# A fused attention and MLP block on one Trainium2 core: another hand-held list for the same program

## The chip, the cores and the metric

The kernel runs on one core of one Trainium2 chip. The metric is the device time of one execution in microseconds (us) on that core; lower is better. Times of several executions are given by their median.

## What is computed

The reference is one pre-norm transformer block on 2048 tokens of width 640, in bfloat16:

```python
x = A_x
h = x + _A_ref(_layernorm(x), A_wq, A_wk, A_wv, A_wo, A_beta)   # attention with a compressive memory
h2 = h + _B_ref(_layernorm(h), B_w1, B_w2)                       # silu MLP, 640 -> 1728 -> 640
```

The attention has 32 heads of 20 elements. The 2048 tokens are cut into 4 segments of 512. Within a segment each head does causal softmax attention; beside it, each query reads a memory matrix M (and its normaliser z) that holds all earlier segments, and the two results are mixed with a gate:

```python
for s in range(4):
    p = softmax(qs @ ks.T * scale + mask);  a_dot = p @ vs
    pq = phi(qs);  a_mem = (pq @ M) / (pq @ z + 1e-06)          # phi(t) = t+1 if t>0 else exp(t)
    outs.append(g * a_mem + (1.0 - g) * a_dot)
    pk = phi(ks);  M = M + pk.T @ vs;  z = z + pk.sum()
```

## The kernel before, in words

The program is a graph of some 1,400 small tasks. Each task is a few instructions of one engine, or one DMA, with the tiles that it reads and writes. `build` declares the tasks segment by segment; `schedule` (line 286) then walks one list, `ORDER` (line 356), and gives each task its place, its engine and its buffer slots. An entry reads `name/engine:slots`: `qe020x/A:0` is task `qe020x` on ScalarE with slot 0 of its pool; without an engine the task's first one is taken. `fill30:7` puts 30 matmuls on zeros into PSUM bank 7 that nothing reads. An entry `e10a+` where another list has `e10a0` and `e10a2` does the exponentials of four heads in one instruction instead of two. Nothing reorders later: each engine executes its instructions in the sequence in which their tasks stand in the list, and `Tracker.add` (line 72) adds the semaphore waits that the data need. The list is therefore the whole schedule. It also sets what is queued behind what on SP, which issues nearly all DMAs one after the other: an entry that waits there holds all that come after it.

The names in the list, with the lines that show in the profile (s is the segment 0 to 3, b the block of 128 tokens 0 to 15):

- `x..` loads tokens (L578), `w_..` loads weights (L581; `w_w1_0` to `w_w1_4` are the five 432 KB rows-blocks of the first MLP weight, `w_w2_0` to `w_w2_5` the second weight).
- `n1_st`, `n1_r`, `n1_ap` are the first layer norm of a block: statistics (L742, L745), reciprocal root (L757 to L763) and apply (L769). `n1_tr` is the DMA that transposes the result into `xT` (L798). `n2_..` is the same for the second norm, into `hT`.
- `pr` projects to q or k (PE, L866), `qe` evicts that from PSUM (L882 on ScalarE, L883 on VectorE), `v`/`ve` are the values (PE L827, eviction L842).
- `ex`, `pha`, `phb` make phi (L889, L896, L902). `vt` and `vp` are DMAs that copy parts of q, k and phi(q) into the layout of three extra head groups (L914, L927). The first segment's q and k, and these copies, lie in the space of the second MLP weight, so the profile calls them `w_sb`.
- `qk` are the scores of four heads (PE, L964), `e` their exponentials (ScalarE, L976), `mk` the causal mask (GpSimd, L987), `av` the product with the values (PE, L1008, in segment 0 L1092), `oe` its eviction, `tn` a turn back to token order plus the read of the memory (PE, L1038, L1042, in segment 0 L1123), `nm` the division (VectorE, L1056 to L1062, in segment 0 L1135 to L1137), `ad` the sum (GpSimd, L1070).
- `kt` transposes phi(k) by DMA (L1207), `kg`/`kh` gather it (L1198), `mz`, `ma`, `mb` update the memory (L1225, L1241, L1249).
- `ot` transposes the attention's output by DMA (L1264), `wo` projects it (PE, L1272), `rs` adds it to the tokens (VectorE, L1280).
- `h1`, `th`, `s` are the MLP's first matmul with silu (PE L1307, in the last partial chunk L1301; ScalarE L1316; VectorE L1322), `h2` the second (PE, L1349), `o` the sum (VectorE, L1362), `out` the store (L1367).

PSUM has 8 banks. A matmul that needs a bank waits until the task that read it last is done, so an eviction that stands late in VectorE's or ScalarE's part of the list can hold TensorE. There are 12 token buffers for 16 blocks: `x12` loads the last four blocks into the buffers of the first four, and so waits for the four stores `out0` to `out3`.

The scores run as four matmuls side by side on 20 rows each (`tile_position=(32 * r, 0)`), the product with the values as four on 32 columns each; everything else uses the whole array. The list interleaves these with projections and MLP matmuls, so TensorE changes between the three forms all through the first 240 us.

The lines that place a task:

```python
for row in ORDER:
    name, _, slots = row.partition(":")
    name, _, eng = name.partition("/")
    ...
    t = todo.pop(name)
    t.eng = {"A": AC, "D": DV, "G": PO, "S": SP}[eng] if eng else list(t.engs)[0]
    ...
        a.slot = slots.pop(0)
    ...
    order.append(t)
```

## Time and profile before

| what | value |
|---|---|
| median of 3 runs | 298.06 us (297.7 to 300.65) |
| the profiled execution | 298.33 us, its span 296.6 us |
| TensorE busy | 285.0 us, 96% of the span, 2991 matmuls |
| VectorE, ScalarE, GpSimd busy | 222.8, 217.5, 139.9 us |
| mean granted TensorE clock | 1.000 |
| moved by DMA | 25.40 MB, mean 86 GB/s |

The span is the time from the first to the last instruction; the 1.7 us between it and the execution's own time lie around the program. In the chain of waits each line is a start, a length and what ran or was waited for. In the list of waits a line reads: engine, line and tile that waited, what released it, then total us, number of times, longest. In the instruction rows, the two numbers ahead are start and length, and what stands in brackets is the engine's idle time just before with its releaser. Two matmuls overlap in the profile, so their pitch is read from one start to the next.

### The profile page before, as it was taken

The numbers are of one execution on the slowest core, as the hardware profiler recorded it, in microseconds if no ns is written. First come the engines' busy times: TensorE is split into PE (matmuls) and PEld (weight loads), VectorE is DVE, ScalarE is ACT, GpSimd is POOL, SyncE is SP. The second block draws the span as 40 slices with busy tenths as digits, with TensorE's granted clock in tenths as the row PEclk, the third lists the DMA queues.
The fourth block names the chain that finished last, engine by engine and source line by source line (L and its number), as shares of the span: only waits on it lengthen the run. The fifth ranks groups of instructions, "written<-read, shape, count | busy, mean of one in ns | idle before, by whom it ended". The sixth has DMA issues, their size and how long they took to land.

```text
span 296.6 us, 7437 instructions
## 1 busy us (share of the span) xinstructions
PE 285.0 (96%) x2991; PEld 167.6 (56%) x2991; DVE 222.8 (75%) x506; ACT 217.5 (73%) x266; POOL 139.9 (47%) x257
## 2 busy tenths in 40 slices
PE   7897879999999999999999999999999999999997
PEld 5775445545665455566643444465665457764575
DVE  3897889768989789899678967759967688626522
ACT  5875979999999899999879999788759751014400
POOL 6246834744656477646525656355576620200000
PEclk9999999999999999999999999999999999999999
DMA  7968772804943321254462400154181023220002
GB/s 208 366 209 114 192 105 68 221 18 98 168 89 75 74 39 26 37 111 66 97 140 51 77 1 2 26 75 88 20 102 32 0 59 76 68 67 25 22 22 91
DMA packets 49906, 25.40 MB, mean 86 GB/s; under 512 B 39488, under 2 KB 48032, under 8 KB 49872
## 3 DMA queue, kind: packets, MB, share of 16 engines
q1 hardware_dynamic: 48204, 23.18, 37.3%
q10 hardware_dynamic: 1668, 1.74, 1.9%
q8 instruction: 24, 0.39, 0.6%
q14 instruction: 10, 0.08, 0.1%
HBM read 10.41 MB, written 2.62 MB: 44 GB/s over the span
## 4 chain that ended last, share of the span: by engine, by line
PE 76%; DVE 8%; DMA 7%; ACT 4%; POOL 2%; issue 2%; SPq 1%; DVEq 0%; ACTq 0%
PE ps_all L1349 19%; PE ps_all L1307 15%; PE ps_all L866 12%; PE ps_all L1272 7%; PE ps_all L964 7%; PE ps_all L827 5%; PE ps_all L1008 5%; ACT PT L976 3%; DMA x_tok<-in_A_x_dram 3%; DMA xT<-xn_rot 2%; PE ps_all L1038 1%; DMA w_sb<-w_sb 1%; PE ps_all L1092 1%; PE ps_all L1225 1%; POOL PT L987 1%
## 5 line engine op out<-in xcount | busy, mean ns | idle before, releaser
L976 ACT ACTIVATE PT<-ps_all 128x1024 bf16<-128x1024 f32 (+1 forms) x120 | 153.1, 1310 | 17.7 <-PE ps_all L964 16.5
L987 POOL TENSOR_SCALAR_AFFINE_SELECT PT<-PT 128x512 bf16<-128x512 bf16 x128 | 81.5, 647 | 59.1 <-ACT PT L976 57.0
L1349 PE MATMUL ps_all<-w_sb,sT 128*128 128x320 bf16 (+2 forms) x462 | 64.9, 295 | 0.0
L1307 PE MATMUL ps_all<-hT,w_sb 128*128 128x512 bf16 (+1 forms) x325 | 63.0, 337 | 0.5 <-DVE sT L1322 0.4
L1316 ACT ACTIVATE th<-ps_all 128x512 f32<-128x512 f32 (+2 forms) x70 | 34.0, 505 | 35.1 <-PE ps_all L1307 31.0
L1349 PEld LDWEIGHTS ps_all<-w_sb,sT 128*128 128x128 bf16 x462 | 43.2, 98 | 18.3 <-issue 1.8
L1322 DVE SCALAR_TENSOR_TENSOR sT<-th,ps_all 128x512 bf16<-128x512 f32 (+2 forms) x70 | 37.8, 561 | 17.1 <-ACT th L1316 16.1
L1307 PEld LDWEIGHTS ps_all<-hT,w_sb 128*128 128x128 bf16 x325 | 29.8, 98 | 25.9 <-issue 3.2
L763 POOL TENSOR_TENSOR rst<-rst,eps_c 128x1 f32<-128x1 f32 x32 | 18.4, 579 | 25.1 <-DVE rst L757 23.5
L742 DVE BATCH_NORM_STATS2 stt<-x_tok 128x6 f32<-128x320 bf16 x62 | 27.2, 481 | 1.8 <-DMA x_tok<-in_A_x_dram 1.4
L1362 DVE SCALAR_TENSOR_TENSOR x_tok<-ps_all,x_tok 128x640 bf16<-128x640 f32 (+3 forms) x18 | 13.3, 745 | 16.7 <-PE ps_all L1349 16.6
L1070 POOL TENSOR_TENSOR otok<-on 128x320 bf16<-128x320 bf16 x24 | 19.0, 796 | 11.5 <-DVE on L1062 11.5
L1272 PE MATMUL ps_all<-wo_sb,oT 128*128 128x320 bf16 x160 | 23.8, 299 | 0.0
L883 DVE CAST QK<-ps_all 128x512 bf16<-128x512 f32 x23 | 15.7, 688 | 8.8 <-PE ps_all L866 8.7
L1062 DVE TENSOR_TENSOR on<-ps_all,rd 128x640 bf16<-128x640 f32 x24 | 19.8, 825 | 0.9
L827 PE MATMUL ps_all<-wv_sb,xT 128*128 128x320 bf16 x120 | 18.3, 299 | 1.6 <-DMA xT<-xn_rot 1.3
L1272 PEld LDWEIGHTS ps_all<-wo_sb,oT 128*128 128x128 bf16 x160 | 15.0, 98 | 7.2 <-issue 1.8
L866 PE MATMUL ps_all<-xT,wkr 128*128 128x512 bf16 x75 | 18.7, 380 | 0.0
L866 PE MATMUL ps_all<-xT,wqr 128*128 128x512 bf16 x75 | 18.2, 380 | 0.0
L842 DVE CAST Vx<-ps_all 128x640 bf16<-128x640 f32 x15 | 12.3, 819 | 5.9 <-PE ps_all L827 5.8
L1008 PE MATMUL ps_all<-PT,Vx 128*32 128x512 bf16 (+3 forms) x384 | 16.4, 301 | 0.1
L769 DVE TENSOR_SCALAR xn_rot<-x_tok,mvt,rst 128x640 bf16<-128x640 bf16 x32 | 14.8, 473 | 1.7 <-POOL rst L763 1.0
(106 smaller groups left out, 338.3 us busy)
## 6 DMA issues: line engine op xcount, KB each, us to landing
w_sb<-in_B_w_dram SPq DMA_DIRECT2D x5, 432.0 KB, 6.1
x_tok<-in_A_x_dram SPq DMA_DIRECT2D x3, 640.0 KB, 8.4
w_sb<-in_B_w_dram SPq DMA_DIRECT2D x3, 480.0 KB, 4.4
out_dram<-x_tok ACTq DMA_DIRECT2D x8, 160.0 KB, 1.8
out_dram<-x_tok SPq DMA_DIRECT2D x7, 160.0 KB, 2.0
QKV<-QK SPq DMA_DIRECT2D x12, 72.0 KB
wo_sb<-in_A_wo_dram SPq DMA_DIRECT2D x1, 800.0 KB, 10.0
sT<-in_A_wq_dram SPq DMA_DIRECT2D x2, 320.0 KB, 4.3
```

The source lines that it names most:

```text
L742: T.add(DV, lambda e, hh=hh: e.bn_stats(out=stt[:, s, 6 * hh:6 * hh + 6], in_=xb[:, 320 * hh:320 * hh + 320]), reads=R((xa, xsub)), writes ...
L827: fns.append(lambda e, c=c, hh=hh: e.matmul(bank(ps, hh)[:, 0:320], lhsT=xT_[:, c, 128 * i:128 * i + 128], rhs=wv_sb[:, c, 320 * hh:320 * ...
L866: fns = [lambda e, kc=kc: e.matmul(bank(ps)[:, lo:hi], lhsT=wt[:, kc, c, :], rhs=xT_[:, kc, lo:hi], start=(kc == 0), stop=(kc == NC - 1)) ...
L964: fns.append(lambda e, j=j, o=o, r=r, q0=q0, q1=q1, qa=qa, ka=ka: e.matmul(ps_all[:, o:o + q1 - q0], lhsT=ka[32 * r:32 * r + DH, 128 * j:1 ...
L976: T.add(AC, lambda e: e.activation(out=pt[:, pta.slot, q0:q0 + nq, 0:width], in_=sc3[:, b0:b0 + nq, 0:width], func=ACT.Exp, scale=SCALE), ...
L987: T.add(PO, lambda e: e.affine_select(out=v, in_=v, pattern=[[0, 4], [1, 128]], compare_op=ALU.is_ge, fill=0.0, base=0, channel_multiplier ...
L1008: fns.append(lambda e, j=j, r=r, h=h, pa=pa, pt=pt, co=co, q0=q0, ji=ji: e.matmul(bank(po)[32 * r:32 * r + 32, q0:hi], lhsT=Vx[:, vx.slot, ...
L1272: fns.append(lambda e, c=c, hh=hh: e.matmul(bank(ps, hh)[:, 0:320], lhsT=oT[:, c, 128 * i:128 * i + 128], rhs=wo_sb[:, c, 320 * hh:320 * h ...
L1307: fns = [lambda e, c=c: e.matmul(bank(ps)[:, lo:hi], lhsT=w1_sb[:, c, 128 * f:128 * f + 128], rhs=hT[:, c, lo:hi], start=(c == 0), stop=(c ...
L1316: T.add(AC, lambda e: e.activation(out=th[:, tha.slot, lo:hi], in_=bank(ps)[:, lo:hi], func=ACT.Tanh, scale=0.5), reads=R((ps, [0])), writ ...
L1322: T.add(DV, lambda e: e.scalar_tensor_tensor(out=sT[:, f, lo:hi], in0=th[:, tha.slot, lo:hi], scalar=1.0, in1=bank(ps)[:, lo:hi], op0=ALU. ...
L1349: fns.append(lambda e, f=f, t0=t0, fr=fr, hh=hh, n=n: e.matmul(bank(pa, hh)[:, 0:n], lhsT=sT[:, f, t0:t0 + 128], rhs=w2_sb[:, fr, c0 + 320 ...
```

## The change

`ORDER` is replaced by another list. The tasks are the same, and so is all arithmetic; new are their sequence, the engine of 60 tasks (20 of these are DMAs that change between the queues of SP and ScalarE), the buffer slots, three more exponentials that are done in one instruction instead of two (43 instead of 40), and the filler matmuls behind the last real one (12 instead of 2). Per engine the list leaves 365 tasks on VectorE (377 before), 277 on ScalarE (278), 227 on GpSimd (219). TensorE changes between its three forms 190 times instead of 195. The first lines of the list show it:

```diff
@@ ORDER
-epsg0:0 vpad0 zpad w2z/G:0 fill30:7 warm iota mt mta mtb mm7 x0:0 x1:4 mm0 n1_st1/A:0,0 w_q0:0 w_q1 w_q2 epsc sel
+vpad1:0 zpad fill30:7 warm iota sel x0:0 w2z/G:0 x1:3 w_q0:0 vpad0 n1_st0/D:3,0 epsc n1_st1/A:0 halfc n1_r0/G w_q1
...
```

**SP's queue at the first segment's transposes and MLP weights.** `xT<-xn_rot` are `n1_tr4` and `n1_tr7` here, `hT<-xn_rot` are `n2_tr1` and `n2_tr0`, `w1_sb` are the five weight blocks. Before (ahead of these rows, one weight block, `w_w1_0`, stands in front of the second token load, near the program's start):

```order
L581 DMA w1_sb<-in_B_w1_dram 128x1728
L798 DMA_TRANSPOSE xT<-xn_rot 128x5x128 [waits s_dve]
L581 DMA w1_sb<-in_B_w1_dram 128x1728 x2
L798 DMA_TRANSPOSE xT<-xn_rot 128x5x128 [waits s_dve]
L1264 DMA_TRANSPOSE oT<-otok 128x5x128 [waits s_dve]
L1264 DMA_TRANSPOSE oT<-otok 128x5x128
L581 DMA w1_sb<-in_B_w1_dram 128x1728
L581 DMA w2_sb<-in_B_w2_dram 128x4x640 [waits s_pe,s_act]
L798 DMA_TRANSPOSE hT<-xn_rot 128x5x128 [waits s_dve] x2
L1207 DMA_TRANSPOSE phiKt<-phiK 128x4x128
```

The same place now:

```order
L581 DMA w1_sb<-in_B_w1_dram 128x1728 x2
L798 DMA_TRANSPOSE xT<-xn_rot 128x5x128 [waits s_dve]
L581 DMA w1_sb<-in_B_w1_dram 128x1728
L798 DMA_TRANSPOSE xT<-xn_rot 128x5x128
L1264 DMA_TRANSPOSE oT<-otok 128x5x128 [waits s_dve]
L1264 DMA_TRANSPOSE oT<-otok 128x5x128
L581 DMA w1_sb<-in_B_w1_dram 128x1728
L798 DMA_TRANSPOSE hT<-xn_rot 128x5x128 [waits s_dve]
L1207 DMA_TRANSPOSE phiKt<-phiK 128x4x128 [waits s_dve]
L581 DMA w1_sb<-in_B_w1_dram 128x1728
L798 DMA_TRANSPOSE hT<-xn_rot 128x5x128 [waits s_dve]
L581 DMA w2_sb<-in_B_w2_dram 128x4x640
```

Three weight blocks still stand ahead of `n1_tr7`, but two of them now ahead of `n1_tr4`; the block that was loaded near the start, `w_w1_0`, is now the last and stands between `n2_tr1` and `n2_tr0`.

**VectorE behind the second output projection of segment 0.** L1280 is `rs2`, which frees the PSUM banks that `mz10` (the memory update of segment 1) needs; L1056 to L1062 are `nm8`, L1362 is `o1`. Before:

```order
L1056 TENSOR_TENSOR rd<-ps_all,epsg 128x32 [waits s_pe]
L1061 RECIPROCAL rd<-rd 128x32 [waits s_dve]
L1062 TENSOR_TENSOR on<-ps_all,rd 128x640 [waits s_dve]
L1362 SCALAR_TENSOR_TENSOR x_tok<-ps_all,x_tok 128x640 [waits s_pe]
L902 TENSOR_TENSOR phiK<-phiK,ex 128x512 [waits s_act]
L769 TENSOR_SCALAR xn_rot<-x_tok,mvt,rst 128x640 [waits l_n1_tr11,s_pool]
L896 TENSOR_SCALAR phiQ<-QK 128x512
L1280 TENSOR_TENSOR x_tok<-ps_all,x_tok 128x640 [waits s_pe]
```

The same place now:

```order
L1056 TENSOR_TENSOR rd<-ps_all,epsg 128x32 [waits s_pe]
L1061 RECIPROCAL rd<-rd 128x32 [waits s_dve]
L1062 TENSOR_TENSOR on<-ps_all,rd 128x640 [waits s_dve]
L902 TENSOR_TENSOR phiQ<-phiQ,ex 128x512 [waits s_act]
L1362 SCALAR_TENSOR_TENSOR x_tok<-ps_all,x_tok 128x640 [waits s_pe]
L1280 TENSOR_TENSOR x_tok<-ps_all,x_tok 128x640 [waits s_pe]
```

Three steps (L902, L769, L896) that stood between `o1` and `rs2` no longer do; one other L902 has come ahead of `o1`.

**TensorE at the end of segment 0's MLP.** The L1349 rows are `h2_3`, whose result `o3` stores as `out3`; L1008 is `av18`, L964 with 128x384 is `qk20b`, L1225 is `mz12`. Before:

```order
L964 MATMUL ps_all<-QK 128x512 x4
L1349 MATMUL ps_all<-w_sb,sT 128x320 x14
L1008 MATMUL ps_all<-PT,Vx 32x512 x4
L1008 MATMUL ps_all<-PT,Vx 32x256 x4
L1008 MATMUL ps_all<-PT,Vx 32x384 x4
L1008 MATMUL ps_all<-PT,Vx 32x128 x4
L964 MATMUL ps_all<-QK 128x384 x4
L964 MATMUL ps_all<-QK 128x128 x4
L1349 MATMUL ps_all<-w_sb,sT 128x320 x14
L1225 MATMUL ps_all<-Vx,phiKt 128x84 x4
```

The same place now:

```order
L964 MATMUL ps_all<-QK 128x512 x4
L1349 MATMUL ps_all<-w_sb,sT 128x320 x28
L964 MATMUL ps_all<-QK 128x384 x4
L964 MATMUL ps_all<-QK 128x128 x4
L1008 MATMUL ps_all<-PT,Vx 32x512 x4
L1008 MATMUL ps_all<-PT,Vx 32x256 x4
L1008 MATMUL ps_all<-PT,Vx 32x384 x4
L1008 MATMUL ps_all<-PT,Vx 32x128 x4
```

The 28 matmuls of `h2_3` now stand together, ahead of `qk20b` and `av18`. On SP `x12` still follows `out3`, with two `vp` copies between them.

Also moved, without rows here: `qe101`, an eviction of 128x512, from ScalarE to VectorE, where it now stands with `phb031` (L902) and `qe100` (L883) ahead of `n2_ap0`, while `oe0y` (L1110), which stood there, comes behind it; two steps of statistics (`n1_st11`, `n1_st8`) stand between `ve11` and `ve12` on VectorE; and at the end the last block's middle columns (`h2_15_*_1`) are computed ahead of `h2_13`.

More of the change, by code (lines that the diff above doesn't have):

```diff
@@ new lines @@
+n1_ap7:1 mk0x3_384 ve01/A av0x:2 e4x1+:4 ex041:1 phb001 lsc2 phb021 qk4x20:4 ve02/D e4x2+:2 av2x:3 mk4x1_0 mk0y1_0
+mk4x1_256 lsc3 n1_tr5:0 v11:0 oe0x/D:0 tn0x:2 ex011:0 mk0y1_256 mk4x2_0 mk4x1_384 mk4x2_256 oe2x/D:1 n1_ap4:0 qk4x30:4
+e4x30:3 mk0y1_384 e4x32 nm0x:1 ve11/D:1 n1_st11:2 qk0ya0:0 e0ya+:6 n1_st8:6 n1_tr6 v12:4 kt00:1 av4x:6 mm3 mk4x3_0
+kt02:0 mz00:7 ma00/A:0,4 w_w1_4:0 qk1ya0:0 e1ya2:0 w_w1_3 n1_tr4 w_w1_2 ve12/D oe4x/D:0 tn2x:4 nm2x:0 mk4x3_256
+mk4x3_384 av6x:7 oe6x/D:1 tn4x:6 nm4x:2 mm6 e1ya0 qk2ya0:2 e2ya2:1 zf0 tn6x:7 nm6x:0 e2ya0 n1_tr7 v10:0 ot1:0 ve10/D
```

193 lines of the change are left out of this document (94 added, 99 removed).

## The prediction

> **What bounds the kernel now.** I read the page first, then the chain of waits, then the waits of each engine, and last the DMA windows around the long ones.
>
> ```profile
> PE 285.0 (96%) x2991; PEld 167.6 (56%) x2991; DVE 222.8 (75%) x506; ACT 217.5 (73%) x266; POOL 139.9 (47%) x257
> ...
> q8 instruction: 24, 0.39, 0.6%
> ```
>
> TensorE is the bound: 285.0 us busy, 96% of the span. All matmuls stay, so a new list can win only what TensorE waits (and what its changes of form cost), and can lose any amount. The list of its waits says how little that is:
>
> ```profile
> PE ps_all L964 <- DMA w_sb<-w_sb: 1.6, 1, 1.6
> PE ps_all L827 <- DMA xT<-xn_rot: 1.3, 1, 1.3
> ...
> PE ps_all L964 <- DVE otok L1137: 0.9, 1, 0.9
> ...
> PE ps_all L1123 <- DVE otok L1137: 0.4, 1, 0.4
> PE ps_all L1307 <- DVE sT L1322: 0.4, 1, 0.4
> PE ps_all L1225 <- DVE x_tok L1280: 0.4, 1, 0.4
> ```
>
> These six make 5.0 us, and the first four lie between 26 and 46 us (the same list, cut to that window, has them). The 1.3 is `v13`, which waits for the transpose `n1_tr7`. The chain of waits shows that one's length, and the rows of its line how far that is from the usual:
>
> ```profile
> 35.03 7.37 DMA xT<-xn_rot
> 42.45 1.53 PE ps_all L827 x10
> ```
>
> ```profile
> DMA to landing us min/median/max: 2.5/2.9/7.4
> ```
>
> What held it for 4.5 us more than the median? In the window 40.1 to 41.4 us one instruction block of 16 KB (the q8 row of the page: 24 packets, 0.39 MB) is read, and from then on hardly anything else moves:
>
> ```profile
> GB/s 221 261 570 24 16 16 24 16 16 16 0 0 0 0 0 0 0 0 0 0 0 0 0 0 0 0 0 0 0 0 0 0 0 0 0 0 0 0 0 0
> ...
> q8 instruction: 1, 0.02, 5.6%
> ```
>
> So a TensorE fetch can stand beside a stop of all transfers, for about 1.2 us. That is the effect that the new list is built around. Only two waits of TensorE on a DMA are in the list, and only in the window of the 1.3 did I find a fetch: avoiding the stop is worth at most that.
>
> The Trainium skill, "Runtime: NRT & Kernel Launch", section "Instruction fetch mechanics", says that instructions come in blocks of 16 KiB over a queue of the sequencer's own and that crossing a block's boundary is mostly hidden. The size agrees (0.39 MB in 24); TensorE's own waits agree, since none is put down to a fetch; the row of GB/s does not, as far as other transfers go. Taken at its word the late transpose would be queueing alone, and the sum would be the last rival's 296.4.
>
> **The change part by part.** (1) Changes of form. One excursion from full matmuls to scores and back:
>
> ```profile
> 51.53 0.59 PE L866 MATMUL ps_all<-xT,wqr 128*128 128x512 bf16 x2
> 52.06 0.40 PE L964 MATMUL ps_all<-w_sb 20*128 20x256 bf16 x8
> 52.39 0.82 PE L866 MATMUL ps_all<-xT,wkr 128*128 128x512 bf16 x3
> ```
>
> ```profile
> 179.05 2.16 PE ps_all L866 x10
> ```
>
> Ten matmuls of 512 columns take 2.16, so 0.216 each; from 51.53 to 52.39 are 0.86, of which two such take 0.43 and two groups of 256 columns side by side 0.22. The rest, 0.21, is two changes, 0.10 each. The list has 190 instead of 195: -0.5. None of it hides, since TensorE is the bound.
>
> (2) 24 to 43 us. Three weight blocks stay ahead of `n1_tr7`, now two of them ahead of `n1_tr4`; their bytes are the same, so the transposes come at the end of the same DMA work, and `v13` stands at nearly the same instruction count, so the same fetch should meet them. On VectorE two steps of statistics now stand ahead of `ve12` (L842):
>
> ```profile
> DVE Vx L842 <- PE ps_all L827: 2.2, 3, 1.0
> ```
>
> By the L742 row in (4) they are 2 x 0.89 us; 1.0 of that was idle time (the longest wait of L842 from 26 to 46 us), and `n1_ap7` (0.45 as the L769 row) has moved away, so the chain up to `nm6x`, which holds the task ahead of `v13`, ends at least 0.3 later. `v13`'s wait of 1.3 covers that. If the transpose lands early the cover is gone, and only 1.3 - 0.3 = 1.0 is won. Bounds: -1.0, and +1.3 if a second stop of that length falls there. I take 0, because neither the bytes nor the count moved.
>
> (3) 46 to 79 us. ScalarE has almost no slack here:
>
> ```profile
> 46.00:79.00 33.00, 32.16 (x432) 18.39 (x430) 27.53 (x70) 32.55 (x42) 16.65 (x31) 1.00 0.48 108
> ```
>
> ```profile
> 49.34 0.60 ACT L882 ACTIVATE QK<-ps_all 128x512 bf16<-128x512 f32 x1
> ```
>
> It is busy 32.55 of 33.00 us, TensorE 32.16, so TensorE loses 0.84 in all. `qe101` (0.60) leaves ScalarE and two pairs of exponentials become one instruction each. The gain lies between 0 and 0.84; I take half, -0.4.
>
> (4) The price of that stands on VectorE and on SP, at the start of the MLP:
>
> ```profile
> 46.67 0.89 DVE L742 BATCH_NORM_STATS2 stt<-x_tok 128x6 f32<-128x320 bf16 x2
> ...
> 50.41 0.68 DVE L1110 TENSOR_TENSOR oTs<-ps_all,lsc 128x512 bf16<-128x512 f32 x1
> 51.16 0.45 DVE L769 TENSOR_SCALAR xn_rot<-x_tok,mvt,rst 128x640 bf16<-128x640 bf16 x1
> 51.52 0.42 DVE L902 TENSOR_TENSOR phiK<-phiK,ex 128x512 bf16<-128x512 bf16 x1
> ...
> 53.68 0.69 DVE L883 CAST QK<-ps_all 128x512 bf16<-128x512 f32 x1 [0.23 <-PE ps_all L866]
> ```
>
> ```profile
> 50.38 2.58 SPq L798 DMA_TRANSPOSE hT<-xn_rot  x2
> ```
>
> ```profile
> 56.84 1.26 PE L1307 MATMUL ps_all<-hT,w_sb 128*128 128x256 bf16 x10
> ```
>
> ```profile
> w_sb<-in_B_w_dram SPq DMA_DIRECT2D x5, 432.0 KB, 6.1
> ```
>
> ```profile
> w_sb<-in_B_w_dram SPq DMA_DIRECT2D x1, 432.0 KB, 3.4
> ```
>
> `n2_ap0` (L769 at 51.16) gets 0.42 + 0.69 + 0.69 put ahead of it and 0.68 taken away: it ends at 51.6 + 1.1 = 52.7. On SP the weight block `w_w1_0` goes out just ahead of `n2_tr0`, behind `kt03`, at about 52. A block lands 3.4 us after its issue when alone (window 43 to 44.2), 6.1 in the median: 55.4 to 58.1. `n2_tr0` takes 2.5 at least (the L798 row) from 52.7: 55.2, later if the block's bytes go first. The first MLP matmul, which needs both, started at 56.84 without waiting and would by (3) be ready at about 56.4. Bounds 0 and +1.7; I take +0.3, near the alone row, since no other weight is queued then. Behind that wait stand all later matmuls.
>
> (5) `rs2`. The wait of L1225 for L1280 (0.4 in the list) is here:
>
> ```profile
> 91.11 0.52 DVE L902 TENSOR_TENSOR phiK<-phiK,ex 128x512 bf16<-128x512 bf16 x1
> 91.56 0.46 DVE L769 TENSOR_SCALAR xn_rot<-x_tok,mvt,rst 128x640 bf16<-128x640 bf16 x1
> 91.94 0.67 DVE L896 TENSOR_SCALAR phiQ<-QK 128x512 bf16<-128x512 bf16 x1
> 92.53 0.81 DVE L1280 TENSOR_TENSOR x_tok<-ps_all,x_tok 128x640 bf16<-128x640 f32 x1
> ```
>
> ```profile
> 93.49 0.46 PE L1225 MATMUL ps_all<-Vx,phiKt 128*128 128x84 bf16 x8 [0.37 <-DVE x_tok L1280]
> ```
>
> With the three steps gone from ahead of it and one of 0.42 added, `rs2` is ready to start as soon as its matmuls end, some 0.35 sooner. -0.35, bounds -0.37 and 0.
>
> (6) `x12`.
>
> ```profile
> 148.67 0.73 PE L1008 MATMUL ps_all<-PT,Vx 128*32 128x512 bf16 x16
> ```
>
> ```profile
> 156.47 0.89 DVE L742 BATCH_NORM_STATS2 stt<-x_tok 128x6 f32<-128x320 bf16 x2 [1.39 <-DMA x_tok<-in_A_x_dram]
> ```
>
> VectorE stands 1.39 us until the tokens land, and the silu steps behind it hold TensorE (L1307 <- L1322, 0.4). `o3` is now ready one product (0.73) and one score task (0.33 as in (1)) sooner, and `out3` and `x12` with it: 1.06 of the 1.39 go. -0.4; bounds -0.5 and 0.
>
> (7) The end. Ten more filler matmuls of 256 columns, 0.11 each as in (1), are 1.1 us of TensorE behind the last real one.
>
> ```profile
> 294.12 0.38 PE L619 MATMUL ps_all<-zpad 128*128 128x256 bf16 x2
> ...
> 294.32 0.29 DVE L1362 SCALAR_TENSOR_TENSOR x_tok<-ps_all,x_tok 128x128 bf16<-128x128 f32 x1 [0.20 <-PE ps_all L1349]
> ```
>
> ```profile
> out_dram<-x_tok ACTq DMA_DIRECT2D x1, 32.0 KB, 1.5
> ```
>
> They end near 295.6; the last store cannot land before 294.6 + 1.5 = 296.1. Cost 0; +1.1 if that cover were gone.
>
> (8) The rest. With so many places rearranged, waits of the new list's own must come. The nearest rows are the 0.4 waits above; I put in one, +0.4, with bounds -0.5 and +2.
>
> Sum: -0.5 + 0 - 0.4 + 0.3 - 0.35 - 0.4 + 0 + 0.4 = -0.95. The profiled execution took 298.33 (0.27 above the median): 297.4.
>
> **Rivals.** *The front is won* (faster): the waits of 0.9, 0.4 and 1.3 between 34 and 43 us go together, and the +0.3 does not come: 297.4 - 2.6 - 0.3 = 294.5. For it speaks that the list was made with such stops counted; against it the later `ve12` in (2). It decides at whether `n1_tr7` lands by 40 us. *The fetch meets `n2_tr0`* (slower): in the window 55.9 to 57 us of before stands a fetch:
>
> ```profile
> q8 instruction: 1, 0.02, 5.0%
> ```
>
> It fell at the first MLP matmul, which `n2_tr0` did not hold; now that transpose is later and may be in flight. Price as for `n1_tr7`: 7.4 - 2.9 = 4.5 later, 55.2 becomes 59.7, TensorE stands 3.3 at 56.4: 297.4 - 0.3 + 3.3 = 300.4, and some 0.6 more, what (3) wins and more, as ScalarE, full there, cannot catch up: 301.0. It decides at a landing after 56.4. *Waits change places*: what (3), (5) and (6) win comes back elsewhere, as +0.5 to +2 in (8): 298 to 300, 298.8 as middle. *Fetches cost nothing*: no transfer is stopped by them, `n1_tr7` lands with its queue and (2) gives -1.0: 296.4; the row of GB/s speaks against it.
>
> **How the numbers follow.** Chances: the forecast 0.38 (296.5 to 298.3), places change 0.24, the front won 0.15, the fetch meets `n2_tr0` 0.15, fetches harmless 0.08. The range 294.4 to 300.9 takes in the front's case and leaves out most of the slow one, and the far ends of (8). Bounds for faster and slower are 295.1 and 301.0, 1% of the median, about what a measurement of this kernel tells from no change: 0.16 faster (the front won, nearly all), 0.68 the same, 0.16 slower (the fetch on `n2_tr0`, two thirds, and 0.06 of the places).
>
> **What would show it.** Right: L1225 <- L1280 gone from TensorE's waits; the wait of L742 on `x_tok` under 0.5; `v13` within 0.7 us of 42.45, still behind `xT<-xn_rot`; first L1307 row without an idle bracket over 0.5; TensorE busy share unchanged at 96%. Wrong: a new wait of TensorE of over 1 us behind a transpose or a weight block; ScalarE's share of 46 to 79 us falling with TensorE's; L827 no longer waiting for `xT`.

## The result, and the profile after

The changed kernel takes 300.04 us in the median of 17 executions (298.18 to 301.84), the kernel before 298.06 us in 17 beside them (297.35 to 300.65). The ratio is 1.0064, with a 95% interval of 1.0046 to 1.0082: slower by 0.64%, or 1.9 us. The forecast was 297.4. The time lies inside the range of 294.4 to 300.9, but the sign is the opposite one. The profiled execution has a span of 298.3 us where the kernel before had 296.6, at the same granted clock of 1.00.

The page of the changed kernel, its busy times and instruction blocks:

```profile
span 298.3 us, 7441 instructions
...
PE 284.2 (95%) x2978; PEld 169.3 (57%) x3001; DVE 219.6 (74%) x494; ACT 219.9 (74%) x267; POOL 141.7 (47%) x265
...
q8 instruction: 24, 0.39, 0.5%
q14 instruction: 10, 0.08, 0.1%
```

TensorE has 3001 weight loads but only 2978 matmuls on record, so 23 matmuls are missing from this trace, and the page's 284.2 us are a little low. What counts is what TensorE waits for. Its list of waits, in the changed kernel:

```profile
PE ps_all L1307 <- DVE on L1062: 1.8, 1, 1.8
PE ps_all L964 <- DVE Vx L842: 1.3, 1, 1.3
...
PE ps_all L827 <- ACT PT L976: 0.8, 1, 0.8
...
PE ps_all L1038 <- DMA phiQv<-phiQ: 0.5, 1, 0.5
```

The two DMA waits that led the list before (1.6 on `w_sb`, 1.3 on `xT`) are gone, and so is the 0.4 of L1225 on L1280. In their place stands one wait of 1.8 us that the list before did not have. It is the first MLP product of segment 1, `h1_1_10_0`. Here are the three places where the changed kernel falls behind, in the timeline of TensorE (columns: start, length, line, tiles, count, and the idle time ahead in brackets):

```profile
109.81 0.32 PE L1038 MATMUL ps_all<-Mzb,phiQv 128*128 128x84 bf16 x4 [0.53 <-DMA phiQv<-phiQ]
```

```profile
151.64 1.02 PE L1307 MATMUL ps_all<-hT,w_sb 128*128 128x512 bf16 x4 [1.81 <-DVE on L1062]
```

```profile
173.26 1.24 PE L866 MATMUL ps_all<-xT,wkr 128*128 128x512 bf16 x5 [0.50 <-issue]
```

The name in the second bracket misleads. The first of that task's five matmuls is one of the missing records, so the wait is put down to what ended last by the profile, the division on L1062, and some 0.2 of the 1.81 us is that matmul itself. What the task waited for are the transposes of `hT`: the last of them, `n2_tr7`, landed at 151.29 in this trace, the weight load of the task waited 1.7 us for it (rows below), and two later runs, whose records are whole here, name it: L1307 <- DMA `hT<-xn_rot`. The same products in the kernel before:

```profile
149.33 1.25 PE L1307 MATMUL ps_all<-hT,w_sb 128*128 128x512 bf16 x5
```

Set side by side at equal work of TensorE, the changed kernel is 0.2 us late at 90 us, 0.2 early at 106, 0.6 late at 112, 0.3 late at 146, 1.8 late at 153, 1.2 late at 164 and 1.7 late at 176. From there to the end nothing more is lost or won. So the loss is made in three places, and most of it, 1.5 of the net 1.7, at one, the transposes of segment 1.

These transposes go out on SyncE's queue. The rows of their line, from issue to landing, in the changed kernel (142 to 148 us) and in the kernel before (137 to 146 us):

```profile
L798 SPq DMA_TRANSPOSE hT<-xn_rot x3: 1276/1415/1768, 143.4 to 146.5; - x3
...
who waited for it (us, times):
  PEld ps_all L1307: 1.7, 1
...
DMA to landing us min/median/max: 4.8/5.3/5.6
```

```profile
L798 SPq DMA_TRANSPOSE hT<-xn_rot x4: 1200/1202/1206, 138.1 to 144.6; - x4
...
DMA to landing us min/median/max: 2.6/3.0/4.2
```

Two things differ. The last three leave later than before, by 3.9, 2.7 and 1.9 us in their order, which uses up the 2.1 us that the last one used to be early (landed 147.19, wanted at 149.33). And they take 1.0 to 2.2 us longer each. (The first row's 1768 ns is the issue of `n2_tr5`, on which a TensorE fetch fell; the usual is 1.20 us.) In the stretch from 148.7 to 150.9 us of the changed kernel, in 40 slices of 55 ns each, the bytes show why:

```profile
GB/s 279 400 88 74 70 70 28 0 0 0 0 0 0 9 223 304 509 312 335 5 9 5 9 5 9 9 5 9 9 23 0 0 23 0 23 256 349 349 372 372
...
q14 instruction: 2, 0.02, 6.1%
```

Two transposes are under way in nearly all of it, and yet for 0.4 us and again for 0.9 us next to nothing moves. Each stop lies in a block of instructions being read. Such a read is called a fetch below. q14 reads blocks of 8 KB; the trace does not name their engine, but in the experiments its fetches move when instructions are added on ScalarE, VectorE and GpSimd. The packets of the two reads here came at 148.78 (0.89 us) and 149.59 (1.24 us). A third came at 146.72 (0.63 us), and TensorE's own block (q8, 16 KB) at 143.80 (0.95 us). The kernel before had no q14 block between 136.77 and 150.47 us, when its transposes were in flight, only one of TensorE at 141.54.

The theories put to the test:

- *F*: block fetches of any engine stop the transfers in flight. The changed list moves three fetches onto three transposes that the MLP waits for.
- *Q*: the transposes queue behind one another and behind stores and copies; the fetches stand there by accident.
- *T*: TensorE's fetch alone (143.80) does it.

### The profile page after: what moved, and what is told of

It reads as the page before. It is cut to its first block, busy times and chain, and to the rows that moved or that the text cites. A ratio compares the mean times of both kernels' runs of the same rounds, so it can differ in the third digit from the quotient of the medians.

```text
span 298.3 us, 7441 instructions
## 1 busy us (share of the span) xinstructions
PE 284.2 (95%) x2978; PEld 169.3 (57%) x3001; DVE 219.6 (74%) x494; ACT 219.9 (74%) x267; POOL 141.7 (47%) x265
## 4 chain that ended last, share of the span: by engine, by line
PE 76%; ACT 11%; DVE 5%; DMA 3%; issue 2%; SPq 2%; ACTq 1%; POOL 0%; DVEq 0%
PE ps_all L1349 21%; PE ps_all L1307 17%; ACT PT L976 9%; PE ps_all L866 8%; PE ps_all L1272 7%; PE ps_all L964 7%; PE ps_all L827 6%; PE ps_all L1008 5%; DMA x_tok<-in_A_x_dram 2%; PE ps_all L1038 1%; PE ps_all L1225 1%; PE ps_all L1042 1%; PE ps_all L1301 1%; DVE stt L742 1%; DMA phiQv<-phiQ 1%
## 5 line engine op out<-in xcount | busy, mean ns | idle before, releaser
L1349 PE MATMUL ps_all<-w_sb,sT 128*128 128x320 bf16 (+2 forms) x462 | 64.7, 295 | 0.1
L1307 PE MATMUL ps_all<-hT,w_sb 128*128 128x512 bf16 (+1 forms) x316 | 61.0, 336 | 3.1 <-DVE on L1062 1.8
L1349 PEld LDWEIGHTS ps_all<-w_sb,sT 128*128 128x128 bf16 x462 | 43.3, 98 | 18.4 <-issue 2.0
L1322 DVE SCALAR_TENSOR_TENSOR sT<-th,ps_all 128x512 bf16<-128x512 f32 (+2 forms) x70 | 37.7, 560 | 17.5 <-ACT th L1316 16.8
L1307 PEld LDWEIGHTS ps_all<-hT,w_sb 128*128 128x128 bf16 x325 | 29.8, 98 | 27.3 <-issue 3.3
L742 DVE BATCH_NORM_STATS2 stt<-x_tok 128x6 f32<-128x320 bf16 x62 | 27.1, 480 | 0.3
L1070 POOL TENSOR_TENSOR otok<-on 128x320 bf16<-128x320 bf16 x24 | 19.6, 818 | 13.1 <-DVE on L1062 13.1
L1362 DVE SCALAR_TENSOR_TENSOR x_tok<-ps_all,x_tok 128x640 bf16<-128x640 f32 (+3 forms) x18 | 13.4, 747 | 15.1 <-PE ps_all L1349 15.1
L1062 DVE TENSOR_TENSOR on<-ps_all,rd 128x640 bf16<-128x640 f32 x24 | 19.8, 825 | 0.8
L883 DVE CAST QK<-ps_all 128x512 bf16<-128x512 f32 x23 | 15.6, 687 | 4.9 <-PE ps_all L866 3.2
L827 PE MATMUL ps_all<-wv_sb,xT 128*128 128x320 bf16 x120 | 18.3, 299 | 0.3
L866 PE MATMUL ps_all<-xT,wkr 128*128 128x512 bf16 x68 | 17.2, 379 | 1.3 <-issue 1.0
L769 DVE TENSOR_SCALAR xn_rot<-x_tok,mvt,rst 128x640 bf16<-128x640 bf16 x32 | 15.0, 478 | 4.1 <-POOL rst L763 4.1
L760 POOL TENSOR_TENSOR rst<-mvt,eps_c 128x1 f32<-128x1 f32 x23 | 4.7, 204 | 27.8 <-DVE mvt L745 24.8
L866 PE MATMUL ps_all<-xT,wqr 128*128 128x512 bf16 x68 | 16.9, 380 | 0.4 <-issue 0.2
L1280 DVE TENSOR_TENSOR x_tok<-ps_all,x_tok 128x640 bf16<-128x640 f32 x16 | 13.0, 810 | 5.5 <-PE ps_all L1272 5.4
```

What stands on the lines that cost most here:

```text
L742: T.add(DV, lambda e, hh=hh: e.bn_stats(out=stt[:, s, 6 * hh:6 * hh + 6], in_=xb[:, 320 * hh:320 * hh + 320]), reads=R((xa, xsub)), writes ...
L827: fns.append(lambda e, c=c, hh=hh: e.matmul(bank(ps, hh)[:, 0:320], lhsT=xT_[:, c, 128 * i:128 * i + 128], rhs=wv_sb[:, c, 320 * hh:320 * ...
L866: fns = [lambda e, kc=kc: e.matmul(bank(ps)[:, lo:hi], lhsT=wt[:, kc, c, :], rhs=xT_[:, kc, lo:hi], start=(kc == 0), stop=(kc == NC - 1)) ...
L1062: T.add(DV, lambda e: e.tensor_tensor(out=on[:, ona.slot, :, :].rearrange("p b (x e) -> p b x e", e=DH), in0=v[:, :, :, 0:DH], in1=r2.unsq ...
L1307: fns = [lambda e, c=c: e.matmul(bank(ps)[:, lo:hi], lhsT=w1_sb[:, c, 128 * f:128 * f + 128], rhs=hT[:, c, lo:hi], start=(c == 0), stop=(c ...
L1322: T.add(DV, lambda e: e.scalar_tensor_tensor(out=sT[:, f, lo:hi], in0=th[:, tha.slot, lo:hi], scalar=1.0, in1=bank(ps)[:, lo:hi], op0=ALU. ...
```

## The experiments

Each kernel ran in five rounds, the two lists joined at 138 us in three. Each ratio is to the kernel before, run beside it (298.19, 298.04, 298.38 and 297.97 us in the four groups). Where a kernel has added instructions, they write a scrap tile and nothing reads it. The entries named in the text are matched with the trace by each engine's order.

### Move the fetches of three engines

```diff
+    pad = sb("pad", [128, 37], F32)
+    def padding(name, eng, c0, n):       # n one-column writes of pad on one engine
 ORDER: warm +padA0 (ScalarE, 6) ... n1_st1/A:0 +padA1 (ScalarE, 6)
        sel +padD (VectorE, 12) ... epsg0 +padG (GpSimd, 13)
```

> The changed kernel with 37 tiny instructions added in stretches where their engine stands idle during the first 10 us: 12 on ScalarE, 12 on VectorE, 13 on GpSimd, each writing one column of a scrap tile. Nothing else moves; they shift the point of the list at which each of these three engines has its next block of instructions fetched (in the trace of the changed kernel the three fetches came at 146.72, 148.78 and 149.59 us, 0.63, 0.89 and 1.24 us long). Theory F, that these fetches held the three transposes hT<-xn_rot: they now come before 143 us, the last transpose lands at 149.8 us or before instead of 151.29, the first MLP product of segment 1 waits under 0.4 instead of 1.81, and the time falls by 1.2 to 1.6 to some 298.6. Theory Q, that the transposes queued behind one another and behind the output and phiQv transfers: landings and the wait stay as they were, time 300.0 +- 0.3. Theory T, that TensorE's own fetch at 143.80 did it: as Q, since that fetch is not moved.

298.77 us, ratio 1.0017 (0.9998 to 1.0037). The fetches came at 135.42, 136.85 and 143.08. The same transposes, in that run, and the first MLP product:

```profile
DMA to landing us min/median/max: 3.4/4.4/4.9
```

```profile
150.65 1.02 PE L1322 MATMUL ps_all<-hT,w_sb 128*128 128x512 bf16 x4 [0.50 <-DVE rd L1071]
```

(L1322 is L1307 moved down by the added lines. The task's first matmul is again not on record, and the name in the bracket again not the transfer.) The wait fell from 1.81 to 0.50 and the time by 1.27, at the edge of what F expected; the last transpose landed at 150.30 and not by 149.8. Q and T expected nothing. At equal work the two traces stay within 0.4 us of each other up to 149 us, and 1.3 us are won from there to 153 us, at the transposes. `n2_tr5` still took 4.9 us, now with only a TensorE fetch (144.18) in its way; the two issued behind it took 4.4 and 3.4 with none in theirs.

### Clear the queue instead

```diff
-  e19a2 out2/A h2_3_2 ... phb200 out3/S av18:6 vp29/S:0 e20b0:5 ex240:0 ... vp23/S
+  e19a2 h2_3_2 ... phb200 av18:6 vp29/S:0 e20b0:5 ex240:0 out2/A ... vp23/S out3/S
```

> The changed kernel with only the issue of two output transfers of 160 KB moved: out2 on ScalarE's queue two score steps later (some 149 us instead of 144.34), out3 on SyncE's queue behind two phiQv copies (some 150 instead of 148.17). So between 144 and 149 us the three transposes have the queues almost to themselves, and the fetches stay. Theory Q: transposes land in 2.9 as elsewhere, the last at 149.4 or before, the wait of the first MLP product falls from 1.81 to under 0.4, time -1.2 to -1.6. Theory F: the transposes still land at 150.5 to 151.5, the wait stays over 1.3, time 299.7 to 300.4 (the tokens of x12 may come 0.3 later).

299.21 us, ratio 1.0039 (1.0009 to 1.0068). Its profiled execution took 302.41 us, at a granted clock of 0.994, so its times are read only within itself:

```profile
PE ps_all L1307 <- DVE phiQ L902: 2.0, 1, 2.0
```

```profile
DMA to landing us min/median/max: 2.8/4.4/4.7
```

The wait stayed (2.0), but this is no clean test of Q. The last transpose went out only at 148.00, so that `out2` (148.56 to 152.10) was again under way beside it. The three q14 fetches came at 147.65, 149.91 and 151.42, spread wider than before, and one transpose landed in 2.8. The interval of the time holds both the full loss and a seventh of it. What part the stores have, this run can't tell.

### Issue two of the transposes earlier

```diff
-  n2_st4:1 n2_r4/D n2_st5:0 n2_r5/G ... n2_ap4:1 n2_tr5 n2_r7/G n2_ap7:3 phb230 n2_tr4 n2_tr7
+  n2_st4:1 n2_r7/G n2_ap7:3 n2_tr7 n2_r4/D n2_st5:0 n2_ap4:1 n2_tr4 n2_r5/G ... n2_tr5 phb230
```

> The changed kernel with two of the three transposes (and the LayerNorm steps ahead of them) issued earlier, at some 141 and 142 us instead of 145.18 and 146.50, about as the list before has them. Theories F and Q alike: only one transpose is left in flight behind 144, it lands at 149.3 or before, the wait of the first MLP product falls from 1.81 to under 0.5 and the time by 1.2 to 1.6 to 298.4-298.8: the place carries most of the loss. If the loss is not of this place (what is won here is lost again at the next wait): wait gone, time 300.0 +- 0.3.

300.81 us, ratio 1.0095 (1.0072 to 1.0118): slower still, a miss for both theories and for the third case. The two early transposes landed in 2.5 and 2.6, the one left behind (issued 147.22, with fetches at 149.50, 150.71 and 150.89) in 4.8:

```profile
DMA to landing us min/median/max: 2.5/2.6/2.6
```

```profile
DMA to landing us min/median/max: 4.8/4.8/4.8
```

But `n2_ap7` now stood ahead of the division `nm17` on VectorE and waited for its root from GpSimd, and TensorE paid at the scores behind `nm17`:

```profile
145.15 0.40 PE L964 MATMUL ps_all<-QK 20*128 20x512 bf16 x4 [1.53 <-DVE on L1062]
```

The wait at the MLP fell to 0.28, partly because TensorE came 1.5 later. The lost head start can't be bought back by this move: VectorE has no room for it.

### Fetches onto the transposes of the kernel before

```diff
 ORDER (before): warm +padA (ScalarE, 5) ... n1_ap1:1 +padG (GpSimd, 10)
```

> The kernel before with 5 tiny instructions added on ScalarE and 10 on GpSimd in their idle time of the first 10 us, so that the two fetches of these engines which came at 150.47 and 158.65 us come at some 144 to 147, when the transposes n2_tr4 (142.47 to 145.84) and n2_tr5 (144.56 to 147.19) are in flight. Theory F: the later transpose lands at 148.2 to 149.5 instead of 147.19; since the first MLP product of segment 1 came at 149.33 the time stays, 298.1 +- 0.4. Theory Q: it lands at 147.2 +- 0.4, same time. A time over 299 would say that the added instructions cost something by themselves.

298.39 us, ratio 1.0012 (0.9993 to 1.0031). The two fetches overshot: they came at 137.82 and 141.58 (1.39 us long). The second still fell on the issue of `n2_tr4` (142.20 to 144.43, 2.2 us instead of 1.2), and the transposes landed at 145.91 and 147.81, between what F and Q expected. The aim was missed and the run decides nothing on F. It does show that fifteen such added instructions cost no more than 0.3%.

### Move TensorE's fetches as well

```diff
+  n1_tp1:0 fill9:2 ... n1_ap6:3 fill10:0 v03:2     # fillers of 16 columns, on top of the moved fetches
```

> The run with the moved fetches of ScalarE, VectorE and GpSimd, and besides 19 fillers of 16 columns in two stretches where TensorE waits anyway (9 ahead of the first projection, 10 ahead of v03), so that every later fetch of TensorE comes some 38 instructions, about 1.9 us, earlier. In that run one TensorE fetch came at 144.18 and n2_tr5, issued at 143.68, took 4.9 us to land (148.62); another at 169.60, with n1_tr15 landing at 172.07. Theory F (any fetch holds the transposes in flight, TensorE's too): the fetch comes at some 142.3, n2_tr5 lands by 147.2, the last of the three by 149.6, the wait of the first MLP product falls from 0.50 to 0.1 or less, and the time by 0.3 to 0.7 to some 298.2. Theory Q (what is left of the delay is the queue's): n2_tr5 still takes over 4.5 us, time 298.8 +- 0.3.

298.07 us, ratio 0.9989 (0.9967 to 1.0010); the profiled execution took 297.40, its span 295.6. The three transposes, and TensorE's largest new wait:

```profile
DMA to landing us min/median/max: 2.7/3.0/4.1
```

```profile
88.32 0.33 PE L1054 MATMUL ps_all<-Mzb,phiQ 128*128 128x84 bf16 x4 [0.63 <-DVE x_tok L1296]
```

`n2_tr5` landed at 146.72, the last at 148.90, and the wait at the MLP is 0.13. With nothing moved but the fetches, the changed list is level with the list before. But TensorE's fetch had moved only with the work: it came at 143.10, again 0.45 us behind the issue of `n2_tr5` (142.65), which took 4.1 us instead of 4.9. At equal work the trace wins only 0.15 at the three transposes against after_fetch_moved, but 0.5 near the front, 1.0 at 107 to 110 us and 0.4 at `n1_tr15`, and loses 0.7 at `tn8`. So what TensorE's fetch costs at the three transposes isn't shown here. The new wait of 0.63 looks like the next such meeting: a TensorE fetch at 83.25 (1.37 us long) met the transpose `kt13`, issued at 82.21 and landed at 86.42, and VectorE's steps behind it were late.

### Repair SyncE's queue at 104 us

```diff
-  out1/S n2_tr2 mk14a_0 mk12a_0 vp17/S n2_tr3 mz11:5 out0/S v23:6 vp13/S
+  n2_tr2 mk14a_0 mk12a_0 vp17/S n2_tr3 mz11:5 v23:6 vp13/S out1/S out0/S
```

> The changed kernel with two output transfers (out1, out0) issued behind the phiQv copy vp13 on SyncE's queue instead of ahead of the transposes n2_tr2 and n2_tr3. In the changed kernel n2_tr3 landed at 108.16 and vp13, issued at 107.47, was still out when the product tn13 wanted it (waits 0.24 and 0.53 of TensorE at 107.9 and 109.3). Theory Q here (the loss at 104 to 112 us is SyncE's order, no fetch was in flight before 109.99): n2_tr3 lands at 107.2 to 107.7, tn13 waits under 0.1, and the time falls by 0.5 to 0.75 to some 299.4. If what is won here is lost at the next wait (the three later transposes): both waits gone, the wait of the first MLP product of segment 1 grows from 1.81 to 2.4, time 300.0 +- 0.3.

300.86 us, ratio 1.0073 (1.0045 to 1.0101). Both waits at 108 to 110 us went, as expected of Q for that place, and `n2_tr3` landed at 107.61. Then most of it was lost again (at equal work 0.8 us are won at 106 to 112 us and 0.65 lost at the transposes):

```profile
PE ps_all L1307 <- DMA hT<-xn_rot: 2.5, 1, 2.5
```

```profile
L798 SPq DMA_TRANSPOSE hT<-xn_rot x3: 1285/1785/1867, 142.3 to 145.5; - x3
...
DMA to landing us min/median/max: 5.3/5.4/5.7
```

The last transpose was issued 1.05 us earlier than in the changed kernel (145.45) and landed 0.42 earlier (150.87): the fetches (145.88, 147.72, 148.61, the last two 0.92 and 1.27 long) had moved along with the work and caught it again. The wait of 2.5 fits the second case (2.4); the time is above its 300.0. The executions lie between 298.01 and 302.29, the profiled one took 299.71, and what spreads them is not shown.

### The two lists joined at 138 us

```diff
 late_as_before: ORDER = entries of after up to n2_tr6, then the rest in the order of before
 late_as_after:  ORDER = entries of before up to n2_tr6, then the rest in the order of after
```

> The changed list up to the transpose n2_tr6 (some 138 us), and everything behind it in the order of the list before. If the loss is what the trace says (0.3 to 0.6 up to 138 us, 1.8 at the three transposes, 0.6 won at the tokens, 0.5 lost at n1_tr15): the wait at the three transposes is under 0.4, VectorE's wait for the tokens is back, time 298.4 to 299.1. If the first part already ruins the second (buffers or queues left in another state): over 299.6.

301.54 us, ratio 1.0128 (1.0091 to 1.0165), the second case. The transposes no longer held the MLP, but VectorE and ScalarE, left in another state by the first part, were late for the second:

```profile
140.87 0.32 PE L1038 MATMUL ps_all<-Mzb,phiQ 128*128 128x84 bf16 x4 [0.52 <-ACT PT L976]
...
144.66 1.53 PE L1349 MATMUL ps_all<-w_sb,sT 128*128 128x320 bf16 x10 [1.08 <-DVE on L1062]
```

> The list before up to n2_tr6 (some 138 us), and everything behind it in the order of the changed list. By the trace the second half alone loses 1.8 + 0.5 - 0.6 - 0.3: time 299.2 to 299.8, with a wait of over 1 us at the first MLP product of segment 1 behind one of the three transposes, as the fetches of VectorE, ScalarE and GpSimd still come near 146 to 151. If the loss needs the first half too: 298.1 +- 0.4.

298.35 us, ratio 1.0016 (0.9989 to 1.0043): a miss for what was read off the trace, and the most telling one. The very stretch of the changed list that loses 1.5 us loses nothing here:

```profile
DMA to landing us min/median/max: 3.3/3.5/4.2
```

```profile
150.15 1.03 PE L1308 MATMUL ps_all<-hT,w_sb 128*128 128x512 bf16 x4
```

The order, the queues and the stores are those of the changed kernel (the three transposes leave 0.2 to 0.4 earlier), and Q would have the wait. But behind the first part of the list before, the q14 fetches came at 137.61, 147.65 and 154.96, one in the stretch instead of three. Where they come is set by how many instructions each engine has had from the start. (The profiled execution took 299.80. At its end the last store, issued while a TensorE fetch (294.73, 1.11 us) was under way, took 2.4 us to land, against 1.5 in the changed kernel.)

### One more fetch into that stretch

```diff
 ORDER (late_as_after): n1_ap1:1 +padG (GpSimd, 6)
```

> The list before up to 138 us with the changed list behind it, which measured 298.35 and had one fetch (147.65) in the stretch of the three transposes; 6 tiny instructions are added on GpSimd in its idle time of the first 10 us, so that GpSimd's own fetch, which came at 154.96 in that run, comes at some 146.5 to 150, when n2_tr4 and n2_tr7 (landed 149.12 and 149.56) are in flight. Theory F: the last of them lands at 150.3 to 151.3, the first MLP product of segment 1 (149.96 there, without a wait) waits 0.3 to 1.2, time 298.7 to 299.6. Theory Q: landings and time as in that run, 298.35 +- 0.3.

297.96 us, ratio 0.9995 (0.9970 to 1.0019). The added fetch came, but on top of the other one: 146.79 (0.47 us) and 146.87 (0.37). The two held `n2_tr4` and `n2_tr7` no longer than the one had (4.1 and 3.4 us to landing, against 4.2 and 3.3), and the last landed at 148.72, before the MLP wanted it. F's number was missed. In the changed kernel they came one after another and took 0.63, 0.89 and 1.24.

### TensorE's fetches alone

```diff
+  n1_tp1:0 fill9:2 ... fill10:0 v03:2              # in the changed kernel, no added padding
```

> The changed kernel with the 19 small fillers alone: TensorE's fetches come 1 to 2 us earlier, the three fetches of ScalarE, VectorE and GpSimd stay at 146 to 150. Theory F, all fetches alike: n2_tr5 lands early (by 147.5), but n2_tr4 and n2_tr7 are still held by the three: wait of the first MLP product 0.8 to 1.8, time 299.2 to 299.8. If TensorE's fetch alone does it: wait under 0.3, time 298.4 +- 0.3.

299.87 us, ratio 1.0056 (1.0037 to 1.0075). The time is near what F expected, but by another way than written. `n2_tr5`, with no fetch in its way, landed in 3.4 us instead of 5.3. `n2_tr4` and `n2_tr7` landed at 150.63 and 151.04, but they left 1.7 us later than in the changed kernel and took 3.7 and 2.9 us, as two of the q14 fetches came only at 150.60 and 150.64. The MLP's wait was gone because TensorE came there 1.9 us later. It had waited 0.86 at `tn8` (the meeting with `kt13` again), 0.53 at `mz10` behind `kt12`, and 1.05 at 110 us, where the changed kernel waits 0.77. So the run speaks neither for nor against T; after_fetch_moved does, where TensorE's fetch stayed and most of the wait went.

### The queue's repair, with the fetches moved

```diff
 after_queue_104 with padA0, padA1, padD and padG
```

> The run with the fetches of the three engines moved (298.77), with out1 and out0 behind vp13 on SyncE's queue as in the run in which that alone won two waits (0.24 and 0.53) and lost them again at the transposes of segment 1. If they were lost there only because the fetches hold these transposes to a fixed time: now the gain stays, time 298.0 to 298.3, wait of the first MLP product under 0.7. If the three transposes are late for another reason that follows the earlier work: wait of 0.9 to 1.2, time 298.8 +- 0.3.

297.62 us, ratio 0.9980 (0.9957 to 1.0002), a little below what F expected. This kernel differs from after_queue_104 in 37 tiny instructions at the start of the list, and takes 3.2 us less (by the ratios 1.0073 and 0.9980, each to the kernel before beside it, 2.8). The two traces differ by 1.9: at equal work 2.0 are won at the transposes and 0.45 at `n1_tr15`, and 0.7 lost near the front.

```profile
DMA to landing us min/median/max: 3.4/4.2/4.9
```

```profile
149.78 1.02 PE L1322 MATMUL ps_all<-hT,w_sb 128*128 128x512 bf16 x4 [0.50 <-DVE rd L1071]
```

```profile
171.02 1.24 PE L881 MATMUL ps_all<-xT,wkr 128*128 128x512 bf16 x5
```

The last row is the product that waited 0.50 for `n1_tr15` in the changed kernel (L881 is L866); here it does not wait. It is the best of all kernels by the median, though its interval still touches 1.

### The meeting with `kt13` taken out by hand

```diff
 moved_pe_shift with pha121, phb121, kt12 and vt14 behind rs3
```

> The best version so far (all fetches shifted, 298.07, span 295.6), in which a TensorE fetch at 83.25 met the transpose kt13 (issued 82.21, landed 86.42), so that VectorE stood 1.58 at the step behind it, rs3 came late and tn8 waited 0.63 for it. Here the two copies that wait for kt13 stand behind rs3 on VectorE. Expected by that: tn8's wait gone, 297.3 to 297.7, faster than both lists. If the late copies hold the scores of segment 1 behind them instead: a new wait of 0.5 to 1 us at 88 to 92, time 298.0 to 298.5.

298.23 us, ratio 1.0011 (0.9985 to 1.0037). `tn8` no longer waits; the scores behind it do:

```profile
91.02 0.40 PE L980 MATMUL ps_all<-QK 20*128 20x512 bf16 x4 [0.54 <-ACT PT L992]
```

The second of the two cases: what is taken from one engine's chain is owed by the next.

### TensorE's fetches moved in the kernel before

```diff
 ORDER (before): n1_tp1 +fill9 ... v01 +fill10 qk4x10     # fillers of 16 columns
```

> The list before, unchanged but for 19 fillers of 16 columns in two stretches where TensorE waits anyway (9 ahead of the first projection, 10 ahead of the scores qk4x10), so that each later fetch of TensorE comes some 38 instructions sooner. In the list before the fetch at 40.19 met n1_tr7 (landed 42.40) and v13 waited 1.3 for it. Theory F: that fetch comes at 38 to 38.7, n1_tr7 lands at 41.2 or sooner, v13 waits under 0.6 for it; time 297.0 to 297.6 if no other transfer that is waited for is met, up to 298.4 if the shifted fetches meet others (n2_tr1 and n2_tr0 at 50 to 56, kt13 at 83 to 86). Theory Q: v13 waits as before, 298.1 +- 0.3.

297.98 us, ratio 0.9988 (0.9970 to 1.0006). The fetch of 40.19 came at 38.36, `n1_tr7` landed at 40.98 instead of 42.40 (5.3 us after its issue instead of 7.4), and `v13` did not wait for it any more:

```profile
41.76 1.52 PE L828 MATMUL ps_all<-wv_sb,xT 128*128 128x320 bf16 x10
43.76 0.40 PE L965 MATMUL ps_all<-w_sb 20*128 20x256 bf16 x8 [0.48 <-ACT PT L977]
```

The step is as F has it, and the time does not move. The fillers had cost 0.6 at the front (`qk4x10` started that much later); `v13` then came 0.7 earlier than in the kernel before, a gain of 1.3; the scores behind it waited 0.48 for ScalarE, and from there on the kernel was only 0.1 to 0.3 ahead.

### The last meeting in the best version

```diff
 moved_queue_104 with qk4x30 ... +fill7 qk0ya0            # 7 fillers of 16 columns
```

> The version with the moved fetches and the repaired queue (297.62), with 7 small fillers in a stretch at 35 us where TensorE waits 1.3, so that TensorE's later fetches come some 14 instructions, 0.6 us, sooner. There a TensorE fetch at 143.27 (0.96 long) met n2_tr5, issued at 142.82 and landed at 147.76, and the first MLP product of segment 1 waited 0.50. Theory F: n2_tr5 lands at 146.8 or sooner, that wait falls under 0.15, time 297.1 to 297.4 and so faster than the list before. Theory Q: wait 0.5, time 297.6 +- 0.3.

298.94 us, ratio 1.0023 (1.0005 to 1.0042): both cases missed. TensorE fell behind moved_queue_104 on the way, by 0.7 us at `mz10`, which waited 0.52 for the transpose `kt12`, by 1.1 behind `tn10`, which waited for a division on VectorE, and by 1.3 at 144 us, so the fetch at 144.56 met `n2_tr5` (issued 144.12, landed 149.14) all the same. Here a shift of the fetches by 14 instructions was no shift by 0.6 us.

### The control

```diff
 ORDER (after): oe19/A:0 +padA (ScalarE, 6) ... phb240 +padD (VectorE, 12) ... mb12 +padG (GpSimd, 13)
```

> The control: the changed kernel with 6, 12 and 13 tiny instructions on ScalarE, VectorE and GpSimd as in the run that moved their fetches (which had 12, 12 and 13), but placed at 151 to 153 us, behind the three transposes, so that the fetches at 146 to 150 stay. Theory F: wait of the first MLP product 1.5 to 2.2, time 299.7 to 300.5. If the added instructions themselves won the 1.3 us: 298.8.

300.11 us, ratio 1.0075 (1.0048 to 1.0103). The fetches came at 147.43, 149.73 and 150.28 and the loss stayed. Here the record is whole, and the wait has its right name and length:

```profile
PE ps_all L1321 <- DMA hT<-xn_rot: 1.5, 1, 1.5
```

```profile
DMA to landing us min/median/max: 4.7/4.9/5.5
```

The added instructions win nothing by themselves. Early ones move the fetches and win 1.27 us, late ones don't and win nothing.

## Why the prediction was wrong, point by point

The failed step is (8), the waits of the new list's own: put at +0.4 ("I put in one"), they cost 1.5 at the transposes of segment 1, 0.8 at 108 to 110 us and 0.5 at `n1_tr15` (TensorE's distance at equal work), 2.8 in all, past the upper bound of +2. With 2.8 in place of 0.4 the sum of -0.95 becomes +1.45; between the profiled executions +1.7 was measured. "A new wait of TensorE of over 1 us behind a transpose" was the prediction's own first sign of being wrong. The rival *waits change places*, at 0.24, described what happened, and its 298 to 300 ends at the result; the forecast sized (8) by the 0.4 waits of the list before, whose profile shows none of the new ones. Nearest in mechanism was *the fetch meets `n2_tr0`*: an `hT` transpose that leaves later, a fetch on it, and the first MLP product held. That came about one segment later, with three other fetches, and cost 1.5 where the rival put 3.3. That 300.04 lies in the range is owed to the rival of the waits and not to the sum. Some 0.3 us that the changed kernel won back between 112 and 146 us are not explained.

(1) Changes of form, -0.5: not tested by itself. No run parts the 5 changes from the order.

(2) The front, 0: near in sum (0.2 late at 47 us), by luck, as the mechanism was wrong. "The same fetch should meet" `n1_tr7` is what failed: the fetch came at 38.39 instead of 40.19 in the changed kernel, the transpose landed at 41.00, and L827 waits for no `xT`. The wait of 1.3 went, and the late `ve12` chain that the prediction named took its place:

```profile
35.11 0.40 PE L964 MATMUL ps_all<-w_sb 20*128 20x256 bf16 x8 [1.28 <-DVE Vx L842]
```

`v13` started at 42.23, 0.2 earlier than before. before_pe_shift shows the same from the other side: with only the fetch moved, the transpose is 1.4 earlier and the time the same.

(3) ScalarE from 46 to 79 us, -0.4: not found. Its busy time did fall,

```profile
46.00:79.00 33.00, 31.47 (x425) 18.58 (x430) 27.76 (x69) 30.95 (x37) 17.30 (x41) 1.00 0.58 128
```

from 32.55 to 30.95 us (its column is the fourth pair), but at equal work TensorE was no further ahead at 79 us than at 47. ScalarE was full there in the kernel before, yet TensorE's waits in that stretch name it only once, with 0.2 us. ScalarE's share falling together with TensorE's was one of the prediction's signs of being wrong; TensorE's 31.47 lacks six of the missing records, so this row can't tell whether its share fell too.

(4) `n2_tr0` behind `w_w1_0`, +0.3: nothing was lost there, the lower bound.

(5) `rs2`, -0.35: right. L1225 <- L1280 is gone, and the two traces come some 0.3 closer at that place:

```profile
93.39 0.46 PE L1225 MATMUL ps_all<-Vx,phiKt 128*128 128x84 bf16 x8
```

(6) `x12`, -0.4: right, and a little more came. VectorE no longer waits for the tokens of L742 between 140 and 165 us (1.4 before), and 0.6 us are won between 153 and 164 us. They don't show in the time, as the transposes had just lost more than twice as much.

(7) The end, 0: right. The traces keep their distance from 176 us to the end.

What was missed on the way to (8): the prediction looked for fetches where the *list before* had its waits, and only for TensorE's. The page of before has no wait at these transposes because they were 2.1 us early. The change uses up that margin, by issuing the last one 1.9 us later, and puts three q14 fetches on them. Either alone was harmless: late_as_after has the late issue with one such fetch instead of three (298.35), and in the kernel before a TensorE fetch at 141.54 fell on a transpose that took 4.2 us, and nothing waited for it, because it was early. The fetches that cost most here are not TensorE's.

The Trainium skill, "Runtime: NRT & Kernel Launch", section "Instruction fetch mechanics", says that crossing a block's boundary is mostly hidden. For the engine that fetches the traces agree: no wait of over 0.6 us of TensorE is put down to issue. For the transfers of others in flight they don't: 1.27 us lie between a list and the same list with its fetches elsewhere.

Three things stay open. What share the stores on the queue have at 144 to 150 us (after_outs_away, 1.0009 to 1.0068) is not settled. And the trace does not name the engine of a q14 fetch, so which of the three costs most wasn't told apart. The 0.5 at `n1_tr15` (4.5 us to landing, with a TensorE fetch at 170.54 in its way) had no experiment of its own.

## What to carry to other kernels

When a list is changed, look at the margin of every transfer that something waits for, not only at the waits that the profile shows: a transpose that is 2 us early is no wait, and becomes one when its issue slips and a stop falls on it. Count the instruction blocks of all engines, not of TensorE alone; a handful of empty instructions at the start, where the engines idle, moves them, and is a cheap test of whether a late transfer is the queue's or a fetch's. A gain ahead of such a stop can be worth nothing until the stop is moved: the same repair of a queue gave 300.86 us with the fetches in place (ratio 1.0073) and 297.62 with them moved (0.9980).

## What the runs showed of the hardware

- While an instruction block of 8 KB was read by q14, transfers in flight all but stopped, for 0.4 to 0.9 us (148.7 to 150.9 us of the changed kernel). Not every read does that, and not every stop has a read: over the changed kernel's trace, while a transpose was in flight, under 30 GB/s (in slices of 50 ns) moved in about half of the time in which a block was read, and in about a quarter of the rest. Three transposes with three such reads and one of TensorE among them landed in 4.8 to 5.6 us. With none, one on its own landed in 2.5 to 2.6, and those behind a late one still took up to 4.4 (after_fetch_moved).
- The reads of q14 took 0.31 to 1.39 us. The twelve of over 0.6 us in all traces had other transfers under way, but most reads beside other transfers were short (median 0.37 us). Two at the same moment (146.79 and 146.87) took 0.47 and 0.37.
- The fetches stayed at their instructions, not at their times: when the queue's repair made everything 1.05 us earlier, the fetches came 0.84 to 1.06 earlier too.
- Added one-column writes in idle time cost nothing that could be measured: 1.0012 (0.9993 to 1.0031) with fifteen of them, though two fetches moved with them.
- A TensorE fetch on `n1_tr7` went with a landing 7.4 us after issue; with that fetch 1.8 us earlier it was 5.3 (before_pe_shift).
